# Who synchronises the entry and the exit of a kernel that is one critical section: GpSimd without its drain, in place of SyncE

## The chip, the cores and the metric

The kernel runs on one core of one Trainium2 chip. The metric is device time in microseconds (us), taken on the chip; the profile's span (first to last instruction of the program) is about 1.8 us shorter. Engines in the profile: PE (TensorE), DVE (VectorE), ACT (ScalarE), POOL (GpSimd) and SP (SyncE). A "q" after the name (SPq, POOLq) means the engine's sequencer, which handles branches, semaphores and DMA issues.

## The reference, cut to what matters

One decode step of attention over a long cache, mixed by a sigmoid gate with a small MLP.

```python
def reference(A_x, A_k_cache, A_v_cache, A_wq, A_wo, B_x, B_w1, B_b1, B_w2, B_b2, gate_w):
    g = sigmoid((A_x * gate_w).sum(-1))
    a = attention(A_x, A_k_cache, A_v_cache, A_wq, A_wo)  # 16 heads on 8 KV heads, 65536 keys, head size 256
    b = mlp(layernorm(B_x), B_w1, B_b1, B_w2, B_b2)
    return g * a + (1 - g) * b                            # 1 x 1 x 448, bfloat16
```

K and V are 268 MB each. The profile counts 544 MB read from HBM, so the work is reading two caches once.

## The kernel before: the parts that the change touches

The whole program is written by hand inside one `tile_critical` section: it has its own semaphores, and the framework adds only what stands around the section. SyncE issues all large DMAs and the output's DMA. GpSimd computes a part of the MLP, which it has done by 790 us, and, at the very end, waits until the output has landed.

```python
    def critical():
        do = Order(nc)
        pe, dve, act, pool, sp = nc.tensor, nc.vector, nc.scalar, nc.gpsimd, nc.sync
        ...
        do.dma("sp", vbuf[:, 0:KA * HQ * DH], A_wq[...], writes=["wqa"])   # first DMA of the stream
        ...
        dve.tensor_copy(out=res[0:97, :], in_=acc4[0:97, 0:DQ]).then_inc(s_fd, 1)
        s_out = nc.alloc_semaphore("s_out")
        sp.wait_ge(s_fd, 4)
        sp.dma_start(
            out=out[0, 0].rearrange("(a n) -> a n", a=4), in_=res[0:97:32, :]
        ).then_inc(s_out, 16)
        pool.wait_ge(s_out, 16)

    with tc.tile_critical():
        critical()
```

What the framework puts around the section can be read in the built program. I call the synchronising engine the announcer. At entry it executes a NOP that raises a semaphore, and every engine waits for it in its branch into the section. At exit it raises an announcement, every engine answers with a drain, the announcer collects the answers, and a last NOP of it lets SyncE and then the closing barrier of the program go on. That closing barrier is gathered by GpSimd in both kernels.

The softmax here doesn't subtract the row's maximum and nothing guards it: scores larger than these inputs give would overflow.

## Time and profile before

| Before | Value |
|---|---|
| time, median of 6 runs on the chip of the comparison | 1265.84 us (1265.68 to 1266.03) |
| span of the profiled run | 1263.6 us |
| DMA share and rate, 27 to 1259 us | 1.00, 433 GB/s |
| SyncE's first DMA issue | 0.958 us |
| exit: from the branch that sees the output landed to the closing barrier's gather | 0.396 us |

The page of the kernel before: busy time by engine, then the share and rate of the DMA engines in 40 equal slices (a 9 is 90% or more), and the traffic.

```profile
PE 718.4 (57%) x4296; PEld 275.5 (22%) x4296; DVE 675.1 (53%) x462; ACT 50.1 (4%) x127; POOL 78.5 (6%) x111
...
DMA  9999999999999999999999999999999999999998
GB/s 405 427 434 433 438 438 422 439 435 431 439 430 428 436 433 438 435 428 433 434 434 438 430 434 434 429 439 427 434 442 429 434 434 432 436 433 430 439 433 354
...
HBM read 544.22 MB, written 0.00 MB: 431 GB/s over the span
```

The DMA engines are busy from beginning to end and no compute engine is above 57%. The same in three stretches (columns: length; busy time and count of PE, weight loads, DVE, ACT, POOL; granted clock; DMA share; GB/s):

```profile
0.00:27.00 27.00, 10.84 (x44) 4.49 (x44) 12.23 (x36) 1.52 (x3) 4.74 (x28) 1.00 0.95 399
27.00:1259.00 1232.00, 706.34 (x4216) 270.23 (x4216) 662.47 (x424) 48.58 (x124) 73.72 (x83) 0.79 1.00 433
1259.00:1264.00 5.00, 1.24 (x36) 0.79 (x36) 0.44 (x2) 0.00 (x0) 0.00 (x0) 0.59 0.02 7
```

So 1232 of 1264 us are a stream of DMA at 433 GB/s. The Trainium skill (DMA: Bandwidth & Descriptors, Anatomy of one DMA) puts the size-dependent part of its fit at 436 GB/s; that fit is for DMAs issued by GpSimd, but this stream from SyncE runs at practically the same rate. Only the first microsecond and the last five can be touched by a change of entry and exit.

The exit, by the view of the exit's line in the kernel before (engine and instruction, count, minimum/median/maximum duration in ns, first and last start in us):

```profile
L815 SPq EVENT_SEMAPHORE  x3: 17/28/28, 1261.6 to 1262.2; - x3
L815 SPq NOP  x2: 13/16/18, 0.7 to 1262.8; - x2
L815 ACTq DRAIN  x1: 8/8/8, 1261.7 to 1261.7; - x1
L815 DVEq DRAIN  x1: 17/17/17, 1261.7 to 1261.7; - x1
L815 PEldq DRAIN  x1: 8/8/8, 1261.7 to 1261.7; - x1
L815 SPq DRAIN  x1: 340/340/340, 1261.7 to 1261.7; - x1
L815 POOLq COMPARE_BRANCH  x1: 33/33/33, 1262.6 to 1262.6; - x1
L815 POOLq DRAIN  x1: 41/41/41, 1262.7 to 1262.7; - x1
```

SyncE announces, and ACT, DVE, PE and SyncE itself drain, a microsecond before GpSimd's branch sees the output at 1262.6. Only GpSimd's own DRAIN and one NOP of SyncE come after. The handshake hides behind the output's DMA.

### The profile page before, as it was taken

What the parts mean: (1) busy time and instruction counts of PE and PEld (TensorE: products, weight loads), DVE (VectorE), ACT (ScalarE), POOL (GpSimd) and SP (SyncE); (2) the same over time, 40 slices, a digit from 0 to 9 for tenths busy, and PEclk for the clock granted to TensorE, in tenths of its full rate; (3) what the DMA queues carried; (4) which work ended last, traced back from release to release, by engine and by line L of the source; (5) the groups of instructions that cost most, each with busy time, mean ns of one, the idle gap of its engine ahead of it and who ended that gap; (6) DMA issues with size and microseconds to landing.
All of it is one profiled execution on the core that took longest, in us unless ns stands there. A gap on an engine that the chain in (4) does not pass through costs nothing. (4 is left out here: it accounts for less than half of the span.)

```text
span 1263.6 us, 10623 instructions
## 1 busy us (share of the span) xinstructions
PE 718.4 (57%) x4296; PEld 275.5 (22%) x4296; DVE 675.1 (53%) x462; ACT 50.1 (4%) x127; POOL 78.5 (6%) x111
## 2 busy tenths in 40 slices
PE   4855655466554665456555565555645656456556
PEld 1311222122221222112221221222212222122212
DVE  5745555465544555455455555464545645465544
ACT  0000000000000000000000000000000000000000
POOL 1001010110110101101111011000000000000000
PEclk9987878778777788778877788777887788777877
DMA  9999999999999999999999999999999999999998
GB/s 405 427 434 433 438 438 422 439 435 431 439 430 428 436 433 438 435 428 433 434 434 438 430 434 434 429 439 427 434 442 429 434 434 432 436 433 430 439 433 354
DMA packets 16840, 544.30 MB, mean 431 GB/s; under 512 B 1856, under 2 KB 3906, under 8 KB 4290
## 3 DMA queue, kind: packets, MB, share of 16 engines
q1 hardware_dynamic: 16744, 544.22, 99.7%
q8 instruction: 2, 0.03, 0.0%
q10 hardware_dynamic: 90, 0.01, 0.0%
q14 instruction: 4, 0.03, 0.0%
HBM read 544.22 MB, written 0.00 MB: 431 GB/s over the span
## 5 line engine op out<-in xcount | busy, mean ns | idle before, releaser
L661 PE MATMUL sc<-kT,qw 128*128 128x512 bf16 x2048 | 571.8, 437 | 488.7 <-PEq L657 488.7
L532 DVE STREAM_TRANSPOSE kT<-kbuf 128x2048 f32<-128x2048 f32 x256 | 572.8, 2285 | 331.7 <-DVEq L524 331.7
L661 PEld LDWEIGHTS sc<-kT,qw 128*128 128x128 bf16 x2048 | 210.4, 108 | 848.7 <-issue 695.5
L675 PE MATMUL pv<-vbuf,pT 128*4 128x512 bf16 x2008 | 120.9, 389 | 27.1 <-PEq L705 26.8
L543 DVE TENSOR_TENSOR og<-pv,og 128x512 f32<-128x512 f32 x40 | 27.7, 692 | 98.8 <-DVEq L524 98.6
L608 ACT ACTIVATE p_t<-sc 128x512 bf16<-128x512 f32 x48 | 28.7, 597 | 1192.2 <-PE sc L661 1192.2
L675 PEld LDWEIGHTS pv<-vbuf,pT 128*4 128x4 bf16 x2008 | 47.2, 88 | 97.2 <-issue 51.7
L589 DVE STREAM_TRANSPOSE pT<-p_t 128x512 bf16<-128x512 bf16 x32 | 22.8, 711 | 74.4 <-DVEq L524 74.4
L635 POOL TENSOR_SCALAR t_b<-t_b 128x448 f32<-128x448 f32 x14 | 7.9, 564 | 360.6 <-ACT t_b L617 360.6
L639 POOL TENSOR_SCALAR t_b<-t_b,hw 128x448 f32<-128x448 f32 x14 | 8.9, 638 | 332.7 <-ACT t_b L625 332.7
L579 DVE STREAM_TRANSPOSE pT<-p_t 128x512 bf16<-128x512 bf16 x8 | 5.7, 711 | 26.9 <-DVEq L524 26.9
L644 POOL TENSOR_TENSOR ymix<-ymix,t_b 128x448 f32<-128x448 f32 x14 | 16.1, 1148 | 1.1
L643 POOL TENSOR_TENSOR t_b<-t_b,u_b 128x448 f32<-128x448 f32 x14 | 15.8, 1126 | 1.2
L638 POOL TENSOR_TENSOR t_b<-t_b,u_b 128x448 f32<-128x448 f32 x14 | 15.8, 1126 | 1.2
L720 PE MATMUL acc<-wo,oT 128*1 128x448 bf16 x28 | 7.9, 413 | 12.7 <-PEq L717 12.7
L542 DVE COPY og<-pv 128x512 f32<-128x512 f32 x8 | 5.5, 692 | 16.1 <-DVEq L524 16.1
L594 DVE STREAM_TRANSPOSE pT<-p_t 128x512 bf16<-128x512 bf16 x8 | 5.7, 711 | 14.9 <-DVEq L524 14.9
L617 ACT ACTIVATE t_b<-h_bc,b1T,w1T 128x448 f32<-128x448 f32 x14 | 10.5, 747 | 0.0
L631 POOL TENSOR_SCALAR u_b<-h_bc,w1T,b1T 128x448 f32<-128x448 f32 x14 | 10.0, 715 | 4.1 <-DVE hw L428 2.7
L608 ACT ACTIVATION_READ_ACCUMULATOR p_t<-sc 128x1 f32 x48 | 9.3, 194 | 0.0
L452 PE MATMUL sc<-vbuf,xw 128*128 128x512 bf16 x32 | 9.2, 456 | 0.0
L685 PEld LDWEIGHTS misc<-mask,og 128*128 128x128 f32 x64 | 8.7, 196 | 2.0 <-DVE og L543 0.9
(86 smaller groups left out, 77.3 us busy)
## 6 DMA issues: line engine op xcount, KB each, us to landing
kbuf<-in_A_k_cache_dram SPq DMA_DIRECT2D x32, 5120.0 KB, 33.2
vbuf<-in_A_v_cache_dram SPq DMA_DIRECT2D x31, 5120.0 KB, 20.6
kbuf<-in_A_k_cache_dram SPq DMA_DIRECT2D x16, 6144.0 KB, 35.5
vbuf<-in_A_v_cache_dram SPq DMA_DIRECT2D x16, 6144.0 KB, 23.8
wo<-in_A_wo_dram SPq DMA_DIRECT2D x7, 448.0 KB, 23.6
vbuf<-in_A_wq_dram SPq DMA_DIRECT2D x1, 3072.0 KB, 10.3
kbuf<-in_A_v_cache_dram SPq DMA_DIRECT2D x1, 2560.0 KB, 25.3
kbuf<-in_A_v_cache_dram SPq DMA_DIRECT2D x1, 1024.0 KB, 27.2
```

Of the source, the lines that this page charges most:

```text
L452: last = e.matmul(q_ps[:], lhsT=xw[:, k, HKV - 1 - n:HKV - 1 - n + 128], rhs=rhs, start=(n == 0 and k == 0), stop=(n == HKV - 1 and k >= K ...
L532: dve.transpose(out=kT[b][:].bitcast(FP32), in_=kn[:, s * SB * 128:(s + 1) * SB * 128]).then_inc(s_kt, 1)
L543: return dve.tensor_tensor(out=og[:], in0=pv[:], in1=og[:], op=ALU.add)
L589: dve.transpose(out=pT[:], in_=p_t[:]).then_inc(s_pt, 1)
L608: ins = act.activation(out=p_t[:], in_=sc[:], func=ACT.Exp, scale=scale, accum_out=den[:, c:c + 1])
L617: ins = act.activation(out=t_b[:], in_=h_bc[:], func=ACT.Square, scale=w1T[:, b:b + 1], bias=b1T[:, b:b + 1],)
L631: lambda: pool.tensor_scalar(out=u_b[:], in0=h_bc[:], scalar1=w1T[:, b:b + 1], scalar2=b1T[:, b:b + 1], op0=ALU.mult, op1=ALU.add,),
L638: lambda: pool.tensor_tensor(out=t_b[:], in0=t_b[:], in1=u_b[:], op=ALU.mult),
L643: lambda: pool.tensor_tensor(out=t_b[:], in0=t_b[:], in1=u_b[:], op=ALU.mult),
L644: lambda: pool.tensor_tensor(out=ymix[:], in0=ymix[:], in1=t_b[:], op=ALU.add),
L661: ins = pe.matmul(sc[:], lhsT=qw[:, q, at:at + 128], rhs=kv[:, :, q // 2, :, q % 2], start=(first and q == 0), stop=(last and q == 7), ski ...
L675: ins = pe.matmul(pv[32 * a:32 * a + 4, :], lhsT=pT[:, k, :, ROW0 + s], rhs=vt[:, j * DH:(j + 2) * DH], start=first and k < 4, stop=last a ...
```

## The change

The intent: let the engine that waits for the output also hold the section, and save its drain.

```diff
-    with tc.tile_critical():
+    with tc.tile_critical(sync_engine=mybir.EngineType.Pool, no_gpsimd_drain=True):
         critical()
```

In the built program the compute instructions of all engines stay the same, in the same order. The entry's NOP moves from SyncE to GpSimd, the announcement and the collecting of answers likewise, and GpSimd's DRAIN at the exit becomes a NOP. The Trainium skill (PSUM — Partial Sum Buffer, Engine vs sequencer instructions) warns that an increment on a NOP says only that earlier instructions were dispatched, where a drain waits for the engine to be idle. Here that loses nothing: each of GpSimd's late operations raises a semaphore of its own, and PE waits for the last of them before it adds the MLP's part.

## The prediction

> **What bounds the kernel.** HBM traffic. The page's DMA row is 9 in 39 of 40 slices, at 431 GB/s over the span; the stretch table gives the DMA engines a share of 1.00 and 433 GB/s from 27 to 1259 us. PE (57%), DVE (53%) and GpSimd (6%) have slack. The kernel is one section that synchronises itself with semaphores; the change touches none of these, only the section's entry and exit. PE, DVE and ACT keep their instructions.
>
> **Entry.** The view of the entry and exit lines shows, after the opening barrier, SyncE's NOP at 0.72 us, which raises a semaphore; all engines wait for it in a branch (0.76 to 0.82 us), SyncE itself at 0.80. Its first DMA issue follows at 0.96 us. In the changed kernel GpSimd, which releases the barrier at 0.61 us, issues this NOP. It should come about 65 to 80 ns after that, at 0.68 to 0.70, and SyncE no longer passes through the NOP: its branch comes at about 0.73 and its first issue at about 0.89. Gain on the critical path, because the DMA stream starts there: about 0.07 us.
>
> **Exit.** Before, SyncE reaches the exit first: it announces at 1261.62 us, right after issuing the output's DMA. ACT, DVE and PE drain at once (8 to 17 ns each), SyncE's own DRAIN takes 340 ns, and its two waits are over at 1262.21. All of it hides behind the output's DMA, whose arrival GpSimd sees only at 1262.58. After that only GpSimd's DRAIN at 1262.74 (41 ns), SyncE's NOP at 1262.81, two short DRAINs and the closing barrier at 1262.98 follow.
> In the changed kernel GpSimd announces, and it is the last to arrive. So everything comes after 1262.58: the announcement at about 1262.74; the four DRAINs of the others at 1262.78 (SyncE's short now, as its DMA is long done); GpSimd's NOP, two waits and NOP at 65 to 80 ns each; then SyncE's DRAIN and the gather, at about 1263.20. The removed drain was worth 41 ns of execution (some 70 to 110 ns with its slot), but a NOP replaces it. Estimate, from these spacings: the end moves out by 0.2 to 0.25 us. The Trainium skill (Perfetto Trace Analysis, Sequencer-only Instruction) says that the profile shows only the execution of such an instruction, not its wait and the travel of its semaphore; the trace agrees: events of 17 ns stand 70 to 80 ns apart. I count spacings, therefore, not durations.
>
> **Sum.** −0.07 + 0.23 = about +0.15 us, 0.01% of 1265.85 us, under the spread of the three runs (0.29 us). A shift of 70 ns at the stream's start may change how transfers meet, by a few tenths.
>
> Predicted 1266.0 us, 8 in 10 between 1265.0 and 1267.0. Chances: faster by over 2% 0.005, within 2% 0.99, slower by over 2% 0.005.
>
> **What would show the steps right or wrong.** Right: SyncE's first DMA issue 0.05 to 0.1 us earlier; no GpSimd DRAIN at the section's end; the announcement from GpSimd after the output's DMA has been seen; from there to the closing barrier's gather about 0.2 us more than before; SyncE's 340 ns DRAIN gone or short; the same GB/s and chain. Wrong: a first issue no earlier; the exit's waits already over when GpSimd arrives; the DMA rate in the middle changed by more than 0.1%.
>
> **What would make it wrong.** A mean DMA rate that settles differently (0.1% is 1.3 us); a GpSimd NOP or event that costs hundreds of ns rather than 70 to 80; SyncE's DRAIN still taking 340 ns behind GpSimd's announcement, which would add about 0.3 us.

## The result, and the profile after

Before: 1265.84 us median (1265.68 to 1266.03, 6 runs). Changed: 1265.97 us median (1265.89 to 1266.03, 6 runs). The outputs are right. The ratio is 1.0001 with a 95% interval of 0.9988 to 1.0014. A ratio here is the mean time of one kernel's runs over that of the other's of the same rounds, so it is not quite the ratio of the medians.

The page and the stretches of the changed kernel:

```profile
PE 720.8 (57%) x4296; PEld 276.2 (22%) x4296; DVE 675.1 (53%) x462; ACT 50.1 (4%) x127; POOL 78.4 (6%) x111
...
DMA  9999999999999999999999999999999999999998
...
HBM read 544.22 MB, written 0.00 MB: 431 GB/s over the span
```

```profile
0.00:27.00 27.00, 11.58 (x44) 4.68 (x44) 12.23 (x36) 1.52 (x3) 4.71 (x28) 0.97 0.95 399
27.00:1259.00 1232.00, 707.94 (x4216) 270.67 (x4216) 662.46 (x424) 48.54 (x124) 73.73 (x83) 0.79 1.00 433
1259.00:1264.00 5.00, 1.31 (x39) 0.81 (x36) 0.44 (x2) 0.00 (x0) 0.00 (x0) 0.50 0.03 10
```

The stream is the same to the last printed digit: 1.00 and 433 GB/s. (PE's clock in the first stretch varies from 0.96 to 1.00 over ten profiles, with either announcer.) The entry, in order of time, first of the kernel before, then of the changed one (start, duration, instruction; in brackets the idle time before it and who ended it):

```profile
0.90 0.52 ACTq L90 DMA_DIRECT2D x_row<-in_A_x_dram  x1
0.94 0.10 POOL L269 MEMSET ident<- 14x14 bf16 x1 [0.50 <-SPq L815]
0.96 0.87 SPq L90 DMA_DIRECT2D vbuf<-in_A_wq_dram  x2
```

```profile
0.89 0.87 SPq L90 DMA_DIRECT2D vbuf<-in_A_wq_dram  x2
0.89 0.53 ACTq L90 DMA_DIRECT2D x_row<-in_A_x_dram  x1
0.97 0.10 POOL L269 MEMSET ident<- 14x14 bf16 x1 [0.53 <-POOLq L815]
```

SyncE's first issue comes 0.07 us earlier; GpSimd, which now executes the NOP, is released 0.03 us later, which nothing waits for. The exit of the changed kernel, by the same view as before:

```profile
L815 POOLq NOP  x3: 13/13/13, 0.7 to 1263.3; - x3
L815 POOLq EVENT_SEMAPHORE  x3: 17/43/43, 1263.0 to 1263.2; - x3
L815 POOLq COMPARE_BRANCH  x1: 33/33/33, 1262.8 to 1262.8; - x1
L815 SPq DRAIN  x1: 7/7/7, 1263.0 to 1263.0; - x1
L815 ACTq DRAIN  x1: 8/8/8, 1263.0 to 1263.0; - x1
L815 DVEq DRAIN  x1: 17/17/17, 1263.0 to 1263.0; - x1
L815 PEldq DRAIN  x1: 8/8/8, 1263.0 to 1263.0; - x1
```

Now GpSimd's branch (1262.8) comes before everything else: announcement, drains and collecting all follow it. SyncE's drain has shrunk from 340 to 7 ns. The trace's records, in ns from the span's start (those before the branch are above the line), set the two exits side by side:

```
before                                     changed
1261619  SyncE   announces                 1262463  the output's last DMA packet ends
1261658  ACT, DVE, PE drain (to 1261665)   -------
1261702  SyncE   DRAIN, 340 ns             1262804  GpSimd  branch: sees the output
1262115  SyncE   collects two answers      1262957  GpSimd  announces
1262184  SyncE   collects two answers      1262999  SyncE, ACT, DVE, PE drain (to 1263011)
1262236  the output's last packet ends     1263057  GpSimd  NOP (in place of its DRAIN)
-------                                    1263150  GpSimd  collects two answers
1262579  GpSimd  branch: sees the output   1263237  GpSimd  collects two answers
1262740  GpSimd  DRAIN, 41 ns              1263323  GpSimd  NOP: section over
1262808  SyncE   NOP: section over         1263362  SyncE   DRAIN
1262880  SyncE   DRAIN                     1263422  SyncE   DRAIN of the barrier
1262944  SyncE   DRAIN of the barrier      1263492  GpSimd  gather
1262975  GpSimd  gather
```

From branch to gather: 396 ns before, 688 ns changed, so +292 ns. From the output's packet to the branch it is 343 and 341 ns, so nothing changed there. The four drains of the changed kernel are over by 1263028 ns, and GpSimd first collects at 1263150; in run 1 below it collects 32 ns after the start of the drain that it waits for. By these spacings GpSimd does not wait for the others here: the 366 ns from its announcement to its last NOP are the spacings of its own instructions, 86 to 100 ns each.

The two profiled spans differ by 512 ns, four times as much as the medians. They split into −66 ns at the first issue, +300 ns from there to the issue of the output's DMA, −9 ns from that issue to the branch, +292 ns of exit and −5 ns of what follows. The +300 ns lie in the stream, which the change does not touch. The experiments had to tell whether that is chance.

### The profile page after: what moved, and what is told of

It reads as the page before. It is cut to its first block, busy times and chain, and to the rows that moved or that the text cites. A ratio compares the mean times of both kernels' runs of the same rounds, so it can differ in the third digit from the quotient of the medians. Undisturbed runs are those within 1.5% of the kernel's fastest.

```text
span 1264.1 us, 10625 instructions
## 1 busy us (share of the span) xinstructions
PE 720.8 (57%) x4296; PEld 276.2 (22%) x4296; DVE 675.1 (53%) x462; ACT 50.1 (4%) x127; POOL 78.4 (6%) x111
```

## The experiments

The theory, A: the exit grew because the announcer is now also the last engine to arrive. Question and answers then stand behind the output, wherever they could hide before. Rivals: B, a handshake collected on GpSimd is slow in itself; C, the drain matters by several tenths of a microsecond; D, such steps do not count in the time. "Exit" below always runs from the branch that sees the output to the closing barrier's gather, and is read from the trace's records.

### 1. GpSimd announces, SyncE waits for the output

```diff
 # against the changed kernel
-        pool.wait_ge(s_out, 16)
+        sp.wait_ge(s_out, 16)
```

> The changed kernel, but SyncE instead of GpSimd waits for the output's DMA, so GpSimd, the announcer, is no longer the last to arrive. Exit = from the start of the branch that sees the output to the closing barrier's gather (0.396 us before, 0.688 us changed). Theory A (the announcer arrives last, so the whole question and answer stands behind the output): exit falls to 0.42 to 0.52 us. Rival B (a handshake collected on GpSimd is slow in itself): exit stays at 0.65 us or more. SyncE's first issue stays at 0.89 us. Time within 0.3 us of the kernel before under both.

Measured: exit 481 ns; first issue at 0.887 us; 1265.76 us median against 1265.79 (ratio 0.9999, 0.9986 to 1.0013). The exit's line in this run:

```profile
L815 POOLq NOP  x3: 13/13/13, 0.7 to 1263.2; - x3
L815 POOLq EVENT_SEMAPHORE  x3: 17/43/43, 789.2 to 1263.1; - x3
L815 ACTq DRAIN  x1: 716/716/716, 1251.4 to 1251.4; - x1
L815 PEldq DRAIN  x1: 398/398/398, 1260.5 to 1260.5; - x1
L815 DVEq DRAIN  x1: 311/311/311, 1260.9 to 1260.9; - x1
L815 SPq COMPARE_BRANCH  x1: 38/38/38, 1262.9 to 1262.9; - x1
L815 SPq DRAIN  x1: 7/7/7, 1263.0 to 1263.0; - x1
```

GpSimd announces already at 789.2 us, when its sequencer has handed out its last operation, and the others drain as they finish. GpSimd still collects, yet 207 ns of the changed kernel's 688 are gone. Theory A holds; B's 0.65 us or more does not.

### 2. SyncE announces and waits for the output

```diff
 # against the kernel before
-        pool.wait_ge(s_out, 16)
+        sp.wait_ge(s_out, 16)
```

> The kernel before, but SyncE, its announcer, waits for the output's DMA. Theory A: SyncE now asks only after the output is seen, exit grows from 0.396 to 0.55 to 0.70 us, and SyncE's 340 ns DRAIN, if it was waiting behind the DMA's issue, becomes short (about 7 ns). Rival B (GpSimd is the slow one): exit stays at 0.40 us or less. If the 340 ns are SyncE's own cost wherever it drains, exit is 0.9 us or more. First issue stays at 0.96 us.

Measured: exit 647 ns; first issue at 0.959 us; 1265.83 us median against 1265.79 (ratio 1.0000, 0.9986 to 1.0014). SyncE's part of the exit's line:

```profile
L815 SPq EVENT_SEMAPHORE  x3: 17/28/28, 1263.1 to 1263.3; - x3
L815 SPq NOP  x2: 18/18/18, 0.7 to 1263.4; - x2
L815 SPq COMPARE_BRANCH  x1: 38/38/38, 1262.9 to 1262.9; - x1
...
L815 SPq DRAIN  x1: 7/7/7, 1263.2 to 1263.2; - x1
```

With the announcer last, the exit grows by 251 ns, and GpSimd collects nothing here. That is A against B from the other side. The 340 ns DRAIN belongs to a drain right behind a DMA issue: about 0.6 us after the output's packet has ended, it is 7 ns.

Together the four exits, in ns:

| Announcer | GpSimd sees the output | SyncE sees the output |
|---|---|---|
| SyncE | 396 (before) | 647 |
| GpSimd, no drain | 688 (changed) | 481 |

An announcer that is last costs 251 ns on SyncE and 207 on GpSimd. GpSimd as announcer costs 85 ns more where the announcer is early, and 41 ns more where it is late. Of the 85 ns, 51 lie between the last engine's drain and the NOP that ends the section, because the answer must first travel to GpSimd and be collected there (in run 1, SyncE's DRAIN at 1263.046 us, GpSimd's wait for it at 1263.078, its NOP at 1263.165). Another 30 lie between that NOP and SyncE's next DRAIN (102 ns against 72): SyncE collects the answers too, its second wait stands at 1263.195, and its DRAIN follows 72 ns later. The kernel before still has GpSimd's drain in its 396 ns; against its 369 ns without the drain (run 3) the 85 ns become 112. So B has a small share; A has the large one.

### 3 and 4. The drain alone: left out with SyncE, kept with GpSimd

```diff
 # sp_nodrain, against the kernel before
-    with tc.tile_critical():
+    with tc.tile_critical(no_gpsimd_drain=True):
 # pool_drain, against the changed kernel
-    with tc.tile_critical(sync_engine=mybir.EngineType.Pool, no_gpsimd_drain=True):
+    with tc.tile_critical(sync_engine=mybir.EngineType.Pool):
```

> The kernel before with only the drain left out (SyncE stays the announcer). Theory A: GpSimd's DRAIN becomes a NOP on the same chain, exit 0.33 to 0.38 us instead of 0.396. Rival C (the drain is what the change was about and costs several tenths): exit 0.25 us or less. Start unchanged, first issue at 0.96 us.

> The changed kernel with its drain kept: GpSimd announces and drains. Theory A: exit 0.70 to 0.78 us, 0.02 to 0.09 over the changed kernel's 0.688. Rival C (leaving out the drain saves several tenths, and without that saving the change would have cost more): exit 0.95 us or more. First issue at 0.89 us as in the changed kernel.

Measured: without the drain and with SyncE, exit 369 ns, 27 less than before, 1265.77 us median against 1265.79 (ratio 1.0000, 0.9987 to 1.0014). With the drain and GpSimd, exit 713 ns, 25 more than changed, 1266.00 us median against 1265.79 (ratio 1.0002, 0.9988 to 1.0015). The exit's line shows the NOP of the first and the DRAIN of the second:

```profile
L815 POOLq NOP  x1: 13/13/13, 1263.1 to 1263.1; - x1
```

```profile
L815 POOLq DRAIN  x1: 46/46/46, 1263.1 to 1263.1; - x1
```

GpSimd's last operation was long done in both, so the drain had nothing to wait for and costs about its 41 to 46 ns less the NOP's 13. C falls for a GpSimd that is done: the drain is worth 25 to 27 ns, in both kernels. What it costs with work in flight was not run.

### 5 and 6. The question and answers by themselves, 16 times

```diff
 # against the kernel before; hs_drain16 has pool.drain() for pool.nop(nofuse=True)
         pool.wait_ge(s_out, 16)
+        for k in range(16):
+            pool.sem_inc(s_an, 1)
+            for eng, s_a in zip((sp, act, pe, dve), s_ans):
+                eng.wait_ge(s_an, k + 1)
+                eng.drain().then_inc(s_a, 1)
+            pool.wait_ge(s_an, k + 1)
+            pool.nop(nofuse=True).then_inc(s_own, 1)
+            for s_a in s_ans:
+                pool.wait_ge(s_a, k + 1)
+            pool.wait_ge(s_own, k + 1)
```

> The kernel before plus 16 rounds of the same question and answer after the output has been seen: GpSimd announces, the four other engines drain and answer, GpSimd collects and goes on. Theory A, from the changed kernel's spacings (announcement at 1262.957, last NOP at 1263.323, one slot more to the next announcement): 0.37 to 0.47 us a round, 6 to 7.5 us in all, in the time as in the span. Rival D (such steps overlap with something after the end and do not count in the time): time grows by under 2 us.

> The same 16 rounds with a GpSimd drain in place of its own answering step. Theory A: 0.03 to 0.1 us a round more, 0.5 to 1.6 us over the run without the drain. Rival C: 0.3 us a round or more, 5 us over it.

Measured: 1272.17 us median against 1265.79 (ratio 1.0051, 1.0035 to 1.0068) without the drain, 1272.29 with it (ratio 1.0053, 1.0036 to 1.0069). The announcements and SyncE's drains of the first run:

```profile
L818 POOLq EVENT_SEMAPHORE  x16: 17/43/43, 1262.8 to 1268.7; - x16
```

```profile
L821 SPq DRAIN  x16: 7/7/7, 1262.8 to 1268.8; - x16
```

Every engine's work is done here, each drain takes 7 to 17 ns, and yet a round takes 375 ns in the records (the second to fourth announcements stand at 1263.129, 1263.504 and 1263.879 us). Thirteen of the 15 intervals between announcements are of 375 ns and the first of 353; the twelfth is of 692 (700 in the run with drains): GpSimd stands 409 ns between two of its waits, where it is 92 in the second to fourth rounds, though all drains are over. Why is not shown. Sixteen rounds of 375 ns and this excess of 317 make 6.32 us. The time grows by 6.38 us, on average 0.40 us a round, so D falls: such steps count in full. The expectation of the drain missed: 0.12 us over the other run, which is 8 ns a round by the medians and also by the records (from the output's packet to the branch that sees the end: 6668 and 6793 ns), where 30 to 100 had been expected. The drain here replaced a step of the same sequencer and had nothing to wait for. (The build folded the NOP into a semaphore instruction, so this is not quite the changed kernel's NOP.)

### 7 and 8. Does the start of the stream reach the end?

```diff
 # against the kernel before; late16 has range(16)
         pe, dve, act, pool, sp = nc.tensor, nc.vector, nc.scalar, nc.gpsimd, nc.sync
+        s_late = nc.alloc_semaphore("s_late")
+        for k in range(64):
+            sp.sem_inc(s_late, 1)
+            sp.wait_ge(s_late, k + 1)
```

> The kernel before with 64 waits of SyncE on its own semaphore ahead of its first DMA issue, about 80 ns each: first issue at about 6.1 us instead of 0.96. If the start of the stream is on the critical path, as the prediction took it, the time grows by the same 5.1 us (4.6 to 5.6). Rival: the stream has slack, or the first transfers are waited for by others anyway, and the time grows by under 3 us.

> The kernel before with 16 waits (instead of 64) ahead of SyncE's first issue: first issue about 1.08 us later, at 2.04 us. Start on the critical path one for one: the output's DMA at 1262.2 us, the time 1.1 us longer (0.9 to 1.3). If a part of about 0.15 us is always absorbed, as 4.32 us of delay gave 4.14 to 4.18, then 0.9 us. If a fixed share of 4% is absorbed, 1.04 us. Rival (the stream absorbs small shifts altogether): under 0.5 us.

The first issue of the stream, in the run with 16 waits and then in the run with 64:

```profile
2.08 0.88 SPq L90 DMA_DIRECT2D vbuf<-in_A_wq_dram  x2
```

```profile
5.28 0.87 SPq L90 DMA_DIRECT2D vbuf<-in_A_wq_dram  x2
```

A wait took 67 to 70 ns, not the 80 that the first expectation assumed, so its delay was 4.32 us, not 5.1. The times grew by 4.18 us (1269.97 against 1265.79; ratio 1.0033, 1.0017 to 1.0050) and, with 16 waits, by 0.97 us for a delay of 1.11 (1266.83 against 1265.86; ratio 1.0008, 0.9992 to 1.0023; the interval contains 1, but all four runs, from 1266.72 up, lie above all nine of the kernel before, up to 1266.18). The issue of the output's DMA moved by 4.14 and 1.11 us against the mean of the six profiles with SyncE as announcer and no delay. So the start of the stream is on the critical path and reaches the end, all of it or nearly all. Whether 0.15 us of it is absorbed, these runs do not resolve.

### 9 and 10. The same kernels again

The kernel before and the changed kernel were each run again, with only a comment added.

> The kernel before once more (a comment added), for the spread: the stretch from the first DMA issue to the last landing of weights in two executions of the same instructions. The profiles of before and changed differ by 0.29 us in that stretch; if that is chance, this run lies 0.1 to 0.5 us from the first one, and exit and first issue repeat within 0.01 us.

> The changed kernel once more (a comment added). First issue at 0.89 us and exit 0.69 us again, within 0.01. Open is whether the 71 ns of earlier first issue reach the end: if they do, the output's DMA is issued near 1261.06 us (the mean of six executions with SyncE as the announcer is 1261.135, less 0.071); if they are lost in the stream, near 1261.14 or later, as in the three executions with GpSimd so far (1261.14 to 1261.22). One run can lie 0.13 us off either way, so it shifts the balance and does not settle it.

Measured: before again, first issue at 0.961 us, exit 397 ns, 1265.81 us median against 1265.79 (ratio 1.0001, 0.9984 to 1.0018). Changed again, first issue at 0.888 us, exit 689 ns, 1266.04 us median against 1265.86 (ratio 1.0001, 0.9988 to 1.0015). Entry and exit repeat within 4 ns. The stream does not: the issue of the output's DMA, in us,

```
SyncE announces (first issue 0.958 to 0.964):  1260.908 1261.131 1261.222 1261.294 1261.090 1261.165   mean 1261.135
GpSimd announces (first issue 0.887 to 0.892): 1261.142 1261.219 1261.207 1261.103                     mean 1261.168
```

The profile of the kernel before that the comparison began with is the earliest of the ten; its second run came 223 ns later with the same program. That first execution's own time, 1265.38 us, is below all 31 timed runs of the kernel before. Most of the +300 ns of the stream can therefore be chance. What is left open is the 72 ns between the means of the first issues (the expectation had 71). If the earlier first issue reached the end, the second mean should lie 72 ns below the first; it lies 33 ns above it. The six values spread by 132 ns (standard deviation), so the difference of means carries about 60 ns (an estimate from that spread and the four's of 54), and this is not settled either way. That a delay of 1.1 us passes through is shown; that a gain of 0.07 us does is not.

No version here beats both kernels in time. By the trace, the kernel before without its drain has the shortest exit, 369 ns, and its 1265.77 us cannot be told from 1265.79.

## Why the prediction was right, point by point

- **The bound.** Right. The stream stayed at 1.00 and 433 GB/s, and the total moved by 0.01%.
- **The entry.** Right as an instruction count: GpSimd's NOP stands at 0.695 us (predicted 0.68 to 0.70), SyncE's branch at 0.734 (0.73), its first issue at 0.892 (0.89). That this gain of 0.07 us arrives at the end was assumed, and is not shown.
- **The exit's mechanism.** Right, and shown by runs 1 and 2: the cost follows whether the announcer is the last to arrive. SyncE's drain became short, as foreseen.
- **The exit's size.** A little low: 0.2 to 0.25 us predicted, 292 ns measured. The mis-sized term is "GpSimd's NOP, two waits and NOP at 65 to 80 ns each": from the announcement on, their starts stand 86 to 100 ns apart, 366 ns for four where 260 to 320 had been counted. The kernel before showed 78 ns between two GpSimd events of 17 ns in the closing barrier and 69 ns between SyncE's two waits for two answers (28 ns each); GpSimd's waits for two answers take 43 ns and stand 87 ns apart. How much of the excess comes from the longer waits is not shown.
- **The drain.** Right in sign: "a NOP replaces it". Its worth is 25 to 27 ns.
- **The sum.** +0.15 us predicted, +0.13 us between the medians. The agreement is better than the terms deserve: the measured terms add up to −72 + 292 = +220 ns, so the small miss of the total is partly luck. Over all runs, the changed kernel has a mean of 1265.99 us (11 runs) and the kernel before 1265.85 us (31 runs; with the four of run 9 the mean is the same), a difference of 0.135 with a standard error of 0.05 (an estimate from their spreads, 0.12 and 0.20, as if the runs were independent; they come from several chips, and within the two comparisons that have the changed kernel the means differ by 0.11 and 0.12). That fits +0.15 and, less well, +0.22. Without any gain at the start it should be near +0.29, three standard errors away; so the times speak for an arrival of at least part of the 72 ns, which the ten profiles do not show. Both intervals of the changed kernel's ratio contain 1, so the timed comparison alone would show nothing.

## What to carry to other kernels

Before moving a synchronisation to another engine, ask who arrives last at it: let an engine that is done early ask and collect, so that only the last arrival's answer stands behind the work that ends the kernel. Here that is a matter of 0.2 to 0.25 us per section exit, invisible next to 1264 us of streaming; in a kernel of a few microseconds or with many sections it would weigh more, which no run here shows. Once the announcer is last, the price lies, by the spacings here, in its own four instructions (366 ns on GpSimd, 307 on SyncE in run 2) and not in the drains of the others. Where a change is worth less than the spread of the runs, compare the records of its own steps over several profiles, which repeat within nanoseconds, and not one pair of spans.

## What the Trainium skill lacked or had wrong

- VectorE: DVE Perf Modes, The DRAIN you can't avoid, describes the short boilerplate drains as about 12 ns, constant, on all engines, and ascribes them to the runtime. It has no word on drains that a framework puts at the exit of a section. The drains here took from 7 to 716 ns, by what stood ahead of them: SyncE's 340 ns right behind a DMA issue and 7 ns later, ACT's 716, PE's 398 and DVE's 311 ns where the announcement had already been made and they drained while their own last work still ran.
- Advanced Engine Details and Errata, Control Flow Timing, gives about 108 ns for a compare-and-branch. It does not say what the figure counts. The branches at this section's entry and exit show 33 ns (ACT, GpSimd), 33 to 38 (SyncE), 47 (DVE) and 179 (PE); from the start of a branch to the start of the next instruction it is 147 to 169 ns on ACT, on SyncE and on GpSimd's exit.
- Perfetto Trace Analysis, Sequencer-only Instruction, explains that waits and the travel of a semaphore are not shown, but gives no sizes there. At the exit's line such instructions show 7 to 46 ns where they have nothing to wait for, and in the exits stand 60 to 92 ns apart on SyncE and, from announcement to last NOP, 86 to 100 ns on GpSimd in the changed kernel; 39 to 54 ns pass from an announcement to the drains of the other engines.
- No page has the price of one round in which one engine asks, all five answer and that one collects: 375 ns in 13 of the 15 intervals between announcements, 0.40 us on average in the time.
- No page says what leaving out GpSimd's drain saves when GpSimd has nothing in flight: 25 to 27 ns at an exit.
